# The head of the first convolution block: a transform spread over products, stores put in other queues, and the order of the last steps before the feed-forward part

## The chip, the cores and the metric

The kernel runs on one core of a Trainium2 chip. The metric is the device time of one execution in microseconds; lower is better. Of the kernel before there are three such times and one profiled execution with its trace. Five engines run side by side, each through its own list of instructions in order: TensorE (PE; its weight loads are shown as PEld), VectorE (DVE), ScalarE (ACT), GpSimd (POOL) and SyncE (SP), which does nothing but issue transfers. Transfers issued on SP run in one hardware queue (q1 in the profile), those issued on GpSimd in another (q0); both run on the same 16 DMA engines.

## The reference

```
x = A_u                                             # 2048 x 576
mod = (silu(c) @ w_mod) -> sa, ca, ga, sb, cb, gb   # six rows of 576
h = layernorm(x) * (1 + ca) + sa
dt = exp(log_dt); A = -exp(log_A_real) + 1j * A_imag; C = (C_real + 1j * C_imag) * dt
K[d, l] = 2 * Re( sum_n C[d, n] * exp(A[d, n] * dt[d] * l) )       # l = 0 .. 2047
y = causal convolution of K and h along the sequence (FFT of 4096) + h * D_skip
x = x + ga * y
h = layernorm(x) * (1 + cb) + sb
x = x + gb * ( relu(h @ w1) @ w2 )                  # 576 -> 4608 -> 576
```

All is float32. The inputs of K are scaled, so that K is not small.

## The kernel before, in words

The 2048 positions are cut into four blocks of 512 (block 0 to 3). A block's convolution is done with transforms of length 1024 over a block and its zero half; a later block adds the products of the earlier blocks' spectra. A block then goes through the second layernorm and the feed-forward part (FFN), in which each weight is split into a high part rounded to the matmul's format and a low part, the remainder.

**Head.** `KGen.first` makes K for block 0. The 576 channels are six groups of 96, g = 0 to 5, each in two halves u of 48. For each group it makes tables `W2` (powers of the step, 32 of them) and `W1` (16 values, made by `doubling`: four doublings by multiplication, the last of them of 8 to 16, m = 8, per half u), and `multiply(g)` runs 192 small matmuls on PE (2 halves x 96; each appears twice in the trace, since a float32 matmul is done in two passes), 32 x 16 each, into `kps`. ACT copies `kps` to `ke`; three groups make one half p of K's columns, which SP stores to `kd` and loads back in another order as `kt`. `W1`, `W2` and the factors `zs` are also stored to memory (`W1d`, `W2d`, `Zd`), where the later blocks' K is made from them (`rest`). `doubling`'s last additions (m = 8) run on GpSimd.

**Convolution of block 0**, `conv0`. The half p = 0 of the columns comes first, then p = 1. For each: `transform` multiplies h with a matrix of cosines and sines on PE (`ps_f`, eight matmuls, each copied by ACT to `ZU` or `Z1`), two butterflies on DVE make the spectrum `U` (`butterfly1` into a tile `W`, `butterfly2` out of it), the same is done for K (`ZK` or `WK`, then `K0` or `K1`), `product` on DVE multiplies the spectra (`Y`), two butterflies back make `V`, and `inverse` on PE (`ps_i`) with the matrix `gc` gives the time values, which DVE adds to x (`x2`) and takes statistics of (`bn_stats`). For p = 0 the second butterfly back is folded into the matmuls, 16 of them instead of 8, and for p = 1 the first butterfly of K is folded into PE (`transform1`, 16 matmuls with `fcK` and its negative `fcKn`). Before a transform of K the skip term `dsk` is added to one row of `kt`. The spectra are stored for later blocks by transfers issued on GpSimd (`Ud`, `Rd`).

**Modulation.** `mod_late` makes `sb`, `cb` and `gb`: for each a weight matrix `wm` of 1.3 MB is loaded on GpSimd's queue into one single buffer, 50 matmul passes (`mps`) use it, ACT copies the row, and PE turns it over (`mpt`). The next `wm` can only be loaded when the matmuls of the one before have read the buffer.

**End of the head.** `norm2` finishes the statistics, DVE and ACT make the normalised h, PE transposes it (`ps_t`), ACT and DVE scale it and split it into high and low parts (`xh`, `xl`, `xs`), and then the FFN's first matmuls (`hps`) run. The FFN's first weights come in as `r` on SP's queue; ACT makes their high part and DVE the low part (`w<-r` on both).

**FFN.** `ffn` walks through 36 slices of the hidden size for each of the four blocks: `first` (14 matmuls into `hps`), ACT and DVE split the result (`hh`, `hl`), `second` (14 matmuls into `acc`). Between them `step` puts in pieces of the next block's convolution, beginning with `rest`, whose tables come back on GpSimd's queue.

**What sets the order.** Instructions that are passed through `kept` or `v` while `pinned` is set stand on their engine in the order in which they are written (each gets a dependency on the one before it on that engine); all others are placed by the scheduler of the tile layer. A wait for another engine or a transfer is placed where data or a buffer needs it. `S(i, ...)` are four buffers for spectra, reused by name; the buffers of tag `kt` are two, which hold in turn `kt` of p = 0, the first and the second temporary `T` of `product`, and `kt` of p = 1.

Of the kernel before, what the change touches and what calls it, by code (L numbers as in the profile page):

```python
# [18 lines left out]
P = 128  # L19
L = 2048  # L20
D = 576
# [25 lines left out]
class KGen:  # L47
# [165 lines left out]
    def doubling(self, g):  # L213
# [4 lines left out]
        for i, m in enumerate((1, 2, 4, 8)):  # L218
# [5 lines left out]
            for u in (slice(0, 1), slice(1, 2)) if m > 2 else (slice(0, 2),):  # L224
# [11 lines left out]
                add = p if m == 8 else v  # L236
# [3 lines left out]
    def products(self, ps, W1, W2, u):  # L240

        for q in range(12):
            for dd in range(4):
                ch = dd * 12 + q
                for r in range(2):
                    self.nc.tensor.matmul(  # L246
                        ps[32 * dd : 32 * dd + 32, 12 * u + q, :],
                        W2[:, r, :, ch],
                        W1[:, u, :, r, ch],
                        start=(r == 0),  # L250
                        stop=(r == 1),
                    )

    def first(self, setup, mod, norm):
# [53 lines left out]
        def multiply(g):  # L308
            kps[g] = self.bank(f"kps_{g}")[:, :384].rearrange("p (q a) -> p q a", a=16)
            for u in range(2):  # L310
                self.products(kps[g], self.W1[g], W2s[g][u], u)
# [35 lines left out]
        multiply(4)  # L347
# [118 lines left out]
class Body:  # L466
# [108 lines left out]
    def mod_weights(self, w, col, eng):  # L575
        v = self.I["w_mod"]
        eng.dma_start(out=w[:, 0:4], in_=v[0:512, col].rearrange("(k p) c -> p k c", p=P))
        eng.dma_start(out=w[:64, 4], in_=v[512:576, col])

# [8 lines left out]
    def mod_late(self):  # L588

        nc, act = self.nc, self.nc.scalar.activation  # L590
# [3 lines left out]
        for i, nm in ((3, "sb"), (4, "cb"), (5, "gb")):  # L594
            w = cv.tile([P, 5, D], F32, tag="wm", bufs=1, name=f"wm_{nm}")
            self.mod_weights(w, slice(i * D, (i + 1) * D), nc.gpsimd)
# [3 lines left out]
            for group in (parts[:4], parts[4:]):  # L600
                for k in range(5):
                    kp = P if k < 4 else 64
                    for r, o, c, n in group:
# [3 lines left out]
                        )  # L607
            row = cv.tile([P, 2 * P], F32, tag="row", bufs=1, name=f"row_{nm}")
# [107 lines left out]
    def transform(self, src, fc, Z):  # L716

        nc = self.nc
        for n2 in (0, 2, 1, 3):
            for c in range(2):  # L720
                ps = self.cps.tile([P, 512], F32, tag="cps", bufs=self.nps, name="ps_f")
                o = ps[:, :PC].rearrange("p (a b) -> p a b", a=4)
                nc.tensor.matmul(o, fc[:, n2, c, :], src(n2), start=True, stop=True)  # L723
# [48 lines left out]
    def norms(self, st, kept):  # L772
# [3 lines left out]
        for i in range(4):  # L776
# [3 lines left out]
            if kept:  # L780
                self.tc.keep_in_program_order(sq)
            rs.append(mv)
# [156 lines left out]
    def norm2(self, s, x2, xp, st=None):  # L939
# [15 lines left out]
        for n2 in range(4):  # L955
            if s == 0 and n2 % 2 == 0:
                nc.vector.tensor_scalar(
                    h2[n2][:, :D], x2[:, n2], rs[n2][:, 0:1], rs[n2][:, 3:4],
                    op0=ALU.subtract, op1=ALU.mult,
                )  # L960
                nc.scalar.activation(h2[n2][:, D:], h2[n2][:, 512:D], AF.Copy)
                continue
            for a, b, c in ((0, D, 0), (512, D, D)):
                nc.scalar.activation(
                    h2[n2][:, c : c + b - a], x2[:, n2, a:b], AF.Identity,
                    scale=rs[n2][:, 3:4], bias=rs[n2][:, 4:5],
                )
# [22 lines left out]
    def conv0(self, ctx, c, kg, first, late):  # L990

        nc, I = self.nc, self.I
# [13 lines left out]

        def load(t, a):
            self.kept(nc.sync.dma_start(out=t, in_=a))

        def stores():  # L1010
            for dst, src in self.held:
                load(dst, src)
            self.held.clear()
# [3 lines left out]
        stores()  # L1017
# [409 lines left out]
```

## Time and profile before

| | |
|---|---|
| time, median of three runs | 1402.68 us (1402.18 to 1404.51) |
| the profiled execution's own time | 1402.97 us |
| span of its trace, first to last instruction | 1401.2 us |
| PE busy | 1233.9 us, 88% of the span |
| DVE busy | 878.3 us, 63% |
| ACT busy | 501.7 us, 36% |
| GpSimd busy | 196.0 us, 14% |
| the first FFN matmul (`hps`) begins | 236.98 us after the span's start |

The profile is read by stage, since the share of an engine over the whole span mixes the head, which has hardly any large matmuls, with the FFN. A row of the timeline gives the start in us, the duration of the merged instructions, the engine, the line, the operation with output and input, their number, and in brackets how long the engine sat idle before it and what ended that idle time. A row of the table by stretches gives the stretch, its length, busy time and number of instructions of PE, PEld, DVE, ACT and POOL, the clock that PE was granted (1.00 is full), the mean busy share of the 16 DMA engines, and GB/s.

### The profile page before, as it was taken

The numbers are of one execution on the slowest core, as the hardware profiler recorded it, in microseconds if no ns is written. First come the engines' busy times: TensorE is split into PE (matmuls) and PEld (weight loads), VectorE is DVE, ScalarE is ACT, GpSimd is POOL, SyncE is SP. The second block draws the span as 40 slices with busy tenths as digits, with TensorE's granted clock in tenths as the row PEclk, the third lists the DMA queues.
The fourth block names the chain that finished last, engine by engine and source line by source line (L and its number), as shares of the span: only waits on it lengthen the run. The fifth ranks groups of instructions, "written<-read, shape, count | busy, mean of one in ns | idle before, by whom it ended". The sixth has DMA issues, their size and how long they took to land. (4 is left out here: it accounts for less than half of the span.)

```text
span 1401.2 us, 25949 instructions
## 1 busy us (share of the span) xinstructions
PE 1233.9 (88%) x10600; PEld 978.8 (70%) x10600; DVE 878.3 (63%) x1352; ACT 501.7 (36%) x1006; POOL 196.0 (14%) x267
## 2 busy tenths in 40 slices
PE   5123677999999987899999989999999999999998
PEld 3123455777777776677777867777887878888886
DVE  5977968999875796658744987253989332101011
ACT  6975224222223412432233323533332353323231
POOL 1877311111111100021011010000000000000000
PEclk9555788999999999899999999999999999999999
DMA  6666778688886947499678995675989656666662
GB/s 190 236 239 217 264 260 314 230 296 310 287 304 219 334 156 282 160 324 376 222 245 314 331 361 174 189 233 174 384 303 325 198 160 204 204 195 198 199 197 78
DMA packets 135766, 346.36 MB, mean 247 GB/s; under 512 B 23456, under 2 KB 23744, under 8 KB 135648
## 3 DMA queue, kind: packets, MB, share of 16 engines
q1 hardware_dynamic: 108688, 222.75, 48.6%
q0 software_dynamic: 26672, 121.37, 23.7%
q8 instruction: 83, 1.36, 0.4%
q10 hardware_dynamic: 288, 0.59, 0.1%
q14 instruction: 35, 0.29, 0.1%
HBM read 263.26 MB, written 81.40 MB: 246 GB/s over the span
## 5 line engine op out<-in xcount | busy, mean ns | idle before, releaser
L1203 PE MATMUL acc<-hh,w 128*128 128x512 f32 x1296 | 429.1, 404 | 6.0 <-DVE w L488 6.0
L1178 PE MATMUL hps<-xh,w 128*128 128x512 f32 x1152 | 397.9, 405 | 0.0
L1184 DVE SCALAR_TENSOR_TENSOR hl<-hps,hh 128x512 fp32r<-128x512 f32 x144 | 98.9, 687 | 323.6 <-ACT hh L1183 323.4
L1203 PEld LDWEIGHTS acc<-hh,w 128*128 128x128 f32 x1296 | 244.5, 190 | 59.6 <-DVE w L488 7.5
L1203 PE MATMUL acc<-hl,w 128*128 128x512 f32 x720 | 280.3, 398 | 0.0
L1178 PEld LDWEIGHTS hps<-xh,w 128*128 128x128 f32 x1152 | 219.3, 191 | 48.2 <-ACT xh L981 0.7
L1178 PE MATMUL hps<-xl,w 128*128 128x512 f32 x576 | 230.0, 399 | 0.2 <-DVE xl L986 0.2
L1183 ACT ACTIVATE hh<-hps 128x512 fp32r<-128x512 f32 x144 | 86.0, 597 | 340.7 <-PE hps L1178 340.7
L1162 ACT ACTIVATE w<-r 128x576 fp32r<-128x576 f32 x144 | 98.7, 686 | 260.4 <-PE acc L1203 220.1
L1203 PEld LDWEIGHTS acc<-hl,w 128*128 128x128 f32 x720 | 136.1, 190 | 28.5
L1178 PEld LDWEIGHTS hps<-xl,w 128*128 128x128 f32 x576 | 110.1, 191 | 24.8 <-DVE xl L986 1.3
L246 PE MATMUL kps<-W,W 128*32 128x16 f32 x2304 | 40.0, 219 | 95.3 <-POOL W L59 59.9
L1153 ACT ACTIVATE w<-r 128x640 fp32r<-128x640 f32 x144 | 105.5, 733 | 39.6 <-DMA L1d<-w 30.4
L1178 PE MATMUL hps<-xs,w 128*128 128x512 f32 x288 | 103.7, 422 | 11.2 <-ACT w L1153 4.8
L246 PEld LDWEIGHTS kps<-W,W 128*32 128x32 f32 x2304 | 37.8, 150 | 98.5 <-POOL W L59 61.2
L421 PEld LDWEIGHTS kps<-W1r,W2r 128*32 128x32 f32 x3456 | 68.0, 146 | 31.1 <-issue 21.6
L488 DVE TENSOR_TENSOR Y<-Y,T 128x1152 f32<-128x1152 f32 x64 | 84.9, 1349 | 0.2
L421 PE MATMUL kps<-W1r,W2r 128*32 128x48 f32 (+2 forms) x3456 | 76.5, 238 | 8.0 <-issue 5.0
L1178 PEld LDWEIGHTS hps<-xs,w 128*128 128x128 f32 x288 | 54.1, 191 | 25.2 <-ACT w L1153 5.2
L488 DVE TENSOR_TENSOR w<-r,w 128x64 fp32r<-128x64 f32 (+2 forms) x108 | 58.2, 571 | 14.1 <-ACT w L1153 11.8
L724 ACT ACTIVATE Z<-ps_f 128x288 f32<-128x288 f32 x104 | 42.2, 409 | 68.1 <-PE ps_f L723 62.7
L931 PE MATMUL ps_i<-V,gc 128*128 128x288 f32 x136 | 43.2, 450 | 13.5 <-DVE x L488 10.1
(201 smaller groups left out, 1360.1 us busy)
## 6 DMA issues: line engine op xcount, KB each, us to landing
r<-in_w_dram SPq DMA_DIRECT2D x144, 320.0 KB, 3.7
r<-in_w_dram SPq DMA_DIRECT2D x144, 288.0 KB, 3.6
w<-L1d SPq DMA_DIRECT2D x108, 320.0 KB, 3.0
w<-L2d SPq DMA_DIRECT2D x108, 288.0 KB, 3.3
W2r<-W2d POOLq DMA_DIRECT2D x18, 1536.0 KB, 10.1
W2d<-W SPq DMA_DIRECT2D x12, 1536.0 KB, 7.7
Ua<-Ud POOLq DMA_DIRECT2D x15, 1152.0 KB, 10.8
W<-W1d POOLq DMA_DIRECT2D x18, 768.0 KB, 9.6
```

Source lines behind the costliest of these rows:

```text
L246: self.nc.tensor.matmul(ps[32 * dd : 32 * dd + 32, 12 * u + q, :], W2[:, r, :, ch], W1[:, u, :, r, ch], start=(r == 0), stop=(r == 1),)
L421: nc.tensor.matmul(ps[32 * dd : 32 * dd + 32, q, :], W2[:, r, :, ch], W1[:, :na, r, ch], start=(r == 0), stop=(r == 1),)
L488: return self.kept(self.nc.vector.tensor_tensor(*args, **kw))
L724: nc.scalar.activation(Z[:, n2, c], ps[:, :PC], AF.Copy)
L931: self.nc.tensor.matmul(ps[:, :PC], a, b, start=(i == 0), stop=(i == len(todo) - 1))
L1153: nc.scalar.activation(w[:, 0], r, AF.Copy)
L1162: nc.scalar.activation(w[:, 0:D], r, AF.Copy)
L1178: nc.tensor.matmul(ps, a, x, start=(i == 0), stop=(i == 13))
L1183: nc.scalar.activation(hh, ps, AF.Relu)
L1184: nc.vector.scalar_tensor_tensor(hl, ps, 0.0, hh, op0=ALU.max, op1=ALU.subtract)
L1203: nc.tensor.matmul(acc[i], a, x, start=(f == 0 and j in (0, 3, 6, 9, 12)), stop=(f == NF - 1 and j in (2, 5, 8, 11, 13)),)
```

## The change

All of it lies in the head and in the first weights of the FFN:

- `doubling` of the last group, g = 5: of the last additions (m = 8) those of the second half (u = 1) go from GpSimd to DVE.
- `multiply(4)` takes a generator `between`: the eight matmuls of K's transform for p = 0 (`ZK`) are put in pairs into the matmuls of group 4 at four places, instead of behind all of them.
- The stores: `W2d` of the last group go on SP behind the load of `kt` of p = 1 (before: ahead of it, behind `kt` of p = 0). `Zd` of the last group and the four `W1d` of groups 4 and 5 go from SP to GpSimd, behind the issue of the last `wm`.
- The loads: `fcKn` and `gcn` wait for the last matmul of `multiply(4)`; `gc` goes behind the load of x; `fcU` and `fcK` go behind the FFN's first weights, and the p = 1 transforms use the copies `early`, loaded before, instead of them.
- The first `wm` is loaded behind the load of `kt` of p = 1 (before: ahead of the butterflies of K0). The skip term of p = 1 is added by GpSimd instead of DVE.
- The spectra of p = 1 get other buffers: `V0` that of `U0`, `Z1` and `U1` the fourth, `K1` the third.
- The inverse of p = 0 and its additions to x stand ahead of the last two butterflies (`W`, `V1`), not behind them.
- The FFN's start is cut in two: the high parts of the first weights (`high1`, `high2`, on ACT) stand ahead of the last butterflies, the low parts (on DVE) behind the normalisation of h.
- The row of `gb` is copied by ACT behind the normalisation instead of ahead of it.

```diff
@@ doubling
-                add = p if m == 8 else v
+                add = p if m == 8 and (g < NG - 1 or u.start == 0) else v
@@ products
-    def products(self, ps, W1, W2, u):
+    def products(self, ps, W1, W2, u, between):
         for q in range(12):
+            if q % 6 == 3:
+                for _ in range(2):
+                    next(between, None)
             for dd in range(4):
...
-        multiply(4)
+        between = yield
+        multiply(4, between)
@@ mod_late
-            self.mod_weights(w, slice(i * D, (i + 1) * D), nc.gpsimd)
+            d = self.wm = self.mod_weights(w, slice(i * D, (i + 1) * D), nc.gpsimd)
+            if i == 3:
+                behind(d)
             yield
...
+            if nm == "gb":
+                yield
             row = cv.tile([P, 2 * P], F32, tag="row", bufs=1, name=f"row_{nm}")
@@ conv0
         kt = [self.load_kt(0, 0)]
-        stores()
-        for t, n in ((self.fcU, "fcu"), (self.fcK, "fck"), (self.gc, "gc")):
-            load(t, I[n])
-        for t, a in zip((fcKn, gcn), I["neg"]):
-            load(t, a)
...
-            self.v(ktv[0:1, 0, :, 0], ktv[0:1, 0, :, 0], dv, op=ALU.add)
+            add = nc.gpsimd.tensor_tensor if p else self.v
+            add(ktv[0:1, 0, :, 0], ktv[0:1, 0, :, 0], dv, op=ALU.add)
...
-        run(self.transform(src_K(0), early[:, 1], ZK))
+        ZKs = self.transform(src_K(0), early[:, 1], ZK, self.kept)
+        first.send(ZKs)
+        run(ZKs)
+        for t, a in zip((fcKn, gcn), I["neg"]):
+            d = load(t, a)
+            behind(d, kg.mm)
...
-        V = S(3, "V0")
+        V = S(0, "V0")
         run(self.butterfly1(Y, V))
         next(first, None)
         kt.append(self.load_kt(0, 1))
+        kt1 = self.ktd
+        sK1 = src_K(1)
         self.cps, self.nps = self.pool(c, "cpsb", space=PSUM), 4
-        Z1 = S(2, "Z1")
-        run(self.transform(lambda n2: hv[:, n2, :, 1], self.fcU, Z1))
+        Z1 = S(3, "Z1")
+        run(self.transform(lambda n2: hv[:, n2, :, 1], early[:, 0], Z1))
+        for dst, src in self.held[:2]:
+            load(dst, src)
         x2 = self.x2[0] = self.x2p[0].tile([P, 4, D], F32, tag="x2", bufs=1, name="x2_0")
         load(x2, I["x"][0].rearrange("n m d -> m n d"))
-        stores()
+        load(self.gc, I["gc"])
+        self.cv = self.pool(c, "cvm")
+        mod = self.mod_late(lambda d: behind(d, kt1))
         next(mod)
...
         run(self.product(Y, K1, U1, True))
-        W = S(2, "W")
-        run(self.butterfly1(Y, W))
-        V1 = S(1, "V1")
-        run(self.butterfly2(W, V1, 1))
...
         back(0, ops)
...
+        next(mod)
+        with tc.issue_after(self.wm.ins):
+            for dst, src in self.held[2:]:
+                nc.gpsimd.dma_start(out=dst, in_=src)
...
+        next(self.start)
+        W = S(3, "W")
+        run(self.butterfly1(Y, W))
+        V1 = S(1, "V1")
+        run(self.butterfly2(W, V1, 1))
...
         back(1, lambda n2: [(g(n2, c), V1[:, n2, c]) for c in range(2)])
```

**PE around the products of group 4** (`kps_2012` before and `kps_2004` now are group 4, `kps_2316` and `kps_2301` group 5; `ps_f<-kt,early` is K's transform for p = 0). Before:

```order
L723 MATMUL ps_f<-h_255,early 128x288 x8
L246 MATMUL kps_2012<-W_4_1810,W_8_1801 32x16 x96
L246 MATMUL kps_2012<-W_4_1810,W_9_1802 32x16 x96
L723 MATMUL ps_f<-kt,early 128x288 x8
L246 MATMUL kps_2316<-W_5_1872,W_10_1863 32x16 x96
L246 MATMUL kps_2316<-W_5_1872,W_11_1864 32x16 x96
L723 MATMUL ps_f<-h_255,fcU 128x288 x8
```

Now:

```order
L735 MATMUL ps_f<-h_255,early 128x288 x8
L250 MATMUL kps_2004<-W_4_1810,W_8_1801 32x16 x24
L735 MATMUL ps_f<-kt,early 128x288 x2
L250 MATMUL kps_2004<-W_4_1810,W_8_1801 32x16 x48
L735 MATMUL ps_f<-kt,early 128x288 x2
L250 MATMUL kps_2004<-W_4_1810,W_8_1801 32x16 x24
L250 MATMUL kps_2004<-W_4_1810,W_9_1802 32x16 x24
L735 MATMUL ps_f<-kt,early 128x288 x2
L250 MATMUL kps_2004<-W_4_1810,W_9_1802 32x16 x48
L735 MATMUL ps_f<-kt,early 128x288 x2
L250 MATMUL kps_2004<-W_4_1810,W_9_1802 32x16 x24
L250 MATMUL kps_2301<-W_5_1872,W_10_1863 32x16 x96
```

The eight transform matmuls have moved from between the groups into group 4, in four pairs, and group 5 follows group 4 directly.

**SP from the load of the first `kt` on.** Before:

```order
L1119 DMA kt<-kd_0_57 128x16x72
L1008 DMA W2d_75<-W_10_1863 128x4x768
L1008 DMA W2d_76<-W_11_1864 128x4x768
L1008 DMA Zd_99<-zs_1910 512x1x48
L1008 DMA Zd_100<-zs_1910 512x1x48
L1008 DMA fcU<-in_fcu_dram 128x1024
L1008 DMA fcK<-in_fck_dram 128x1024
L1008 DMA gc<-in_gc_dram 128x1024
L1008 DMA fcKn<-in_neg_dram 128x512
L1008 DMA gcn<-in_neg_dram 128x512
L358 DMA kd_1_58<-ke_1921 64x1152 x2
L1119 DMA kt<-kd_1_58 128x16x72
```

Now:

```order
L1153 DMA kt<-kd_0_57 128x16x72
L1029 DMA fcKn<-in_neg_dram 128x512
L1029 DMA gcn<-in_neg_dram 128x512
L365 DMA kd_1_58<-ke_1921 64x1152 x2
L1153 DMA kt<-kd_1_58 128x16x72
L1029 DMA W2d_75<-W_10_1863 128x4x768
L1029 DMA W2d_76<-W_11_1864 128x4x768
L1029 DMA x_0_2531<-in_x_dram 128x4x576
L1029 DMA gc<-in_gc_dram 128x1024
L1171 DMA r_2725<-in_w_dram 128x640
L1171 DMA r_2727<-in_w_dram 128x640
L1175 DMA r_2729<-in_w_dram 128x576
```

The two `W2d` stores and `gc` now stand behind the second `kt`, and the `Zd`, `fcU` and `fcK` are gone from here. The `W1d` stores, which stood behind the load of x on SP, now stand on GpSimd:

```order
L585 DMA wm_gb<-in_w_mod_dram 64x576
L1123 DMA Zd_99<-zs_1910 512x1x48
L1123 DMA Zd_100<-zs_1910 512x1x48
L1123 DMA W1d_85<-W_4_1810 128x2x768
L1123 DMA W1d_86<-W_4_1810 128x2x768
L1123 DMA W1d_87<-W_5_1872 128x2x768
L1123 DMA W1d_88<-W_5_1872 128x2x768
L386 DMA W_0_2925<-W1d_77 128x2x768
L387 DMA Zr_2926<-Zd_89 128x192
L388 DMA W2r_2924<-W2d_65 128x4x768
```

On GpSimd they stand between the last `wm` and the first loads of `rest`, which before followed each other.

More of the change, by code (lines that the diff above doesn't have):

```diff
@@ L1072, in conv0 @@
         WK = S(1, "WK")
-        run(self.transform1(src_K(1), self.fcK, fcKn, WK))
+        run(self.transform1(sK1, early[:, 1], fcKn, WK))
         next(mod)
@@ L1240, in ffn @@
         low1(1)
+        high1(0)
+        high2(0)
+        high1(1)
+        yield
         split1(0)
```

106 lines of the change are left out of this document (63 added, 43 removed).

## The prediction

> **What bounds the kernel now.** I read the table by stretches first, to find where PE is not the limit, and then the timelines of that place.
>
> ```profile
> 64.00:89.00 25.00, 12.79 (x766) 12.15 (x760) 19.05 (x46) 16.80 (x34) 22.53 (x30) 0.50 0.51 192
> 148.00:162.00 14.00, 4.83 (x267) 4.53 (x268) 13.79 (x27) 0.00 (x0) 6.65 (x7) 0.59 0.96 365
> 195.00:219.00 24.00, 18.96 (x116) 13.64 (x116) 16.22 (x22) 5.68 (x15) 2.93 (x5) 1.00 1.03 398
> 300.00:400.00 100.00, 98.46 (x1549) 79.10 (x1548) 94.30 (x101) 24.26 (x45) 12.85 (x19) 1.00 0.85 297
> ```
>
> In the FFN PE is the limit (98.46 of 100 us), and its work does not change. So the time follows the instant at which the FFN starts, as long as nothing behind it is late. In the head it is DVE that is nearly always busy (13.79 of 14 us), and at 195 to 219 the DMA engines are full at 398 GB/s. DVE's timeline of the head:
>
> ```profile
> 160.91 4.78 DVE L488 TENSOR_TENSOR W<-ZU 128x576 f32<-128x576 f32 x4
> 169.39 1.43 DVE L488 TENSOR_TENSOR W<-ZK 128x576 f32<-128x576 f32 x2 [0.54 <-ACT ZK L724]
> 171.89 1.43 DVE L488 TENSOR_TENSOR W<-ZK 128x576 f32<-128x576 f32 x2 [1.08 <-ACT ZK L724]
> ...
> 176.18 2.62 DVE L488 TENSOR_TENSOR Y<-K,U 128x1152 f32<-128x1152 f32 x2
> ...
> 180.09 1.36 DVE L488 TENSOR_TENSOR Y<-Y,T 128x1152 f32<-128x1152 f32 x1
> ...
> 184.15 2.76 DVE L488 TENSOR_TENSOR V<-Y 128x576 f32<-128x576 f32 x4
> 188.38 1.43 DVE L488 TENSOR_TENSOR W<-Z 128x576 f32<-128x576 f32 x2 [1.47 <-ACT Z L724]
> 191.74 1.43 DVE L488 TENSOR_TENSOR W<-Z 128x576 f32<-128x576 f32 x2 [1.93 <-ACT Z L724]
> ...
> 196.02 0.44 DVE L488 TENSOR_TENSOR kt<-kt,dsk 1x288 f32<-1x288 f32 x1
> 204.07 2.90 DVE L488 TENSOR_TENSOR K<-WK 128x576 f32<-128x576 f32 x6 [7.61 <-ACT WK L763]
> ...
> 214.99 2.76 DVE L488 TENSOR_TENSOR W<-Y 128x576 f32<-128x576 f32 x4
> ...
> 220.60 0.45 DVE L488 TENSOR_TENSOR x<-ps_i,x 128x288 f32<-128x288 f32 x1
> ...
> 224.01 2.28 DVE L488 TENSOR_TENSOR w<-r,w 128x640 fp32r<-128x640 f32 x4
> ...
> 229.32 0.41 DVE L1103 BATCH_NORM_STATS2 st<-x 128x6 f32<-128x288 f32 x1
> 234.13 0.81 DVE L977 TENSOR_SCALAR xf<-ps_t,m_cb,m_sb 128x512 f32<-128x512 f32 x1 [2.25 <-PE ps_t L972]
> ```
>
> The chain is DVE's own work and five waits: 0.54 + 1.08 for `ZK`, 1.47 + 1.93 for `Z1`, 7.61 for `WK`, 12.6 us in sum. The last one is a loop: the skip term is added only at 196.02, behind U1 on DVE, and only then can PE transform K.
>
> **Step 1, the products on PE.** The rows from PE, and those that follow from it on SP:
>
> ```profile
> 67.83 2.18 PE L246 MATMUL kps<-W,W 128*32 128x16 f32 x128 [1.39 <-issue]
> ...
> 150.31 0.30 PE L246 MATMUL kps<-W,W 128*32 128x16 f32 x2 [4.18 <-POOL W L59]
> ...
> 157.76 2.18 PE L246 MATMUL kps<-W,W 128*32 128x16 f32 x127 [4.15 <-issue]
> ...
> 165.39 6.02 PE L723 MATMUL ps_f<-kt,early 128*128 128x288 f32 x16
> 171.34 4.03 PE L246 MATMUL kps<-W,W 128*32 128x16 f32 x249
> ...
> 181.21 0.43 PE L246 MATMUL kps<-W,W 128*32 128x16 f32 x7 [2.12 <-issue]
> ```
> ```profile
> 182.19 1.12 SPq L358 DMA_DIRECT2D kd<-ke  x2
> 185.33 0.38 SPq L1119 DMA_DIRECT2D kt<-kd  x1
> ```
>
> Group 4 takes 15.1 us (150.31 to 165.39), of which 6.5 are work (384 passes at 2.18/128); after each 128 passes PE stands without a releaser. That gap is 4.15 us here, with the DMA engines at 0.96, and 1.39 at 67.83, where they are at 0.51. I read it as PE's instructions arriving by DMA. Now `W2d`, `Zd`, `fcU`, `fcK` and `gc`, some 5 MB by their shapes, leave this stretch, so a lot of 128 should cost about 3.6 us (2.18 + 1.39), and the eight transform matmuls (6.0 us) fill the gaps: the first 140 passes by 153.6, then 4.2 + 6.0 of work, group 4 and `ZK` done at about 164 instead of 171.4. Group 5 then takes its 10.3 us (171.34 to 181.64) and ends at 174.3, 7.3 us earlier. Bounds: 5 us of gain if only the transform's 6.0 hide, 9 if gaps vanish; none if the gaps stay and the pairs add to them. The Trainium skill ("Runtime: NRT & Kernel Launch", Instruction fetch mechanics) has fetching in blocks of 256 instructions, mostly hidden. The lots of 128 matmuls with 128 weight loads agree with the block; the 4.15 us do not agree with "hidden".
>
> **Step 2, DVE to U1.** The moved additions cost DVE two of 0.5 us, about 1.1 in all. They give back the slow `W<-ZU`: 4.78 us where the same shape takes 2.76 (184.15), because GpSimd ran at the same time:
>
> ```profile
> 159.48 4.92 POOL L59 TENSOR_TENSOR W<-T,T 128x384 f32<-128x384 f32 x4 [6.09 <-issue]
> ```
>
> Half of GpSimd's four are gone, so 2.0 less. The `ZK` waits (1.6) go. Y starts at 176.18 - 2.5 = 173.7 (a gain between 1 and 3). The copy `cb` moves within the same path. `Z1` no longer waits for the buffer that V0's butterfly reads, and its matmuls follow group 5 (from 174.3), so the 1.47 + 1.93 go too: U1 ends at 196.02 - 5.9 = 190.1.
>
> **Step 3, K1.** The new waits first: SP now waits for group 4's last matmul ahead of `fcKn`; behind it stand `gcn` and the stores of `ke`, which need group 5 anyway, so it costs nothing unless group 4 ends after group 5's copy, which cannot be. GpSimd waits for `kt` of p = 1; behind it stand the first `wm` and U1's store, which pay in step 4.
>
> `kt` of p = 1 is issued 3.7 us after group 5 (181.64 to 185.33): 178.0. It also needs its buffer, the first `T`, read by the row at 180.09: 181.4 - 2.5 = 178.9 now. So this, not PE, decides, which makes step 1 forgiving by a microsecond.
>
> ```profile
> kt<-kd SPq DMA_DIRECT2D x2, 576.0 KB, 4.1
> wm_sb<-in_w_mod_dram POOLq DMA_DIRECT2D x1, 1152.0 KB, 6.1
> wm_cb<-in_w_mod_dram POOLq DMA_DIRECT2D x1, 1152.0 KB, 10.8
> ```
> ```profile
> 196.56 0.72 PE L760 MATMUL ps_f<-kt,fcK 128*128 128x288 f32 x2 [2.14 <-DVE kt L488]
> ...
> 207.55 0.66 PE L931 MATMUL ps_i<-V,gc 128*128 128x288 f32 x2
> ...
> 216.20 0.65 PE L931 MATMUL ps_i<-V,gcn 128*128 128x288 f32 x2
> ...
> 221.10 5.84 PE L931 MATMUL ps_i<-V,gc 128*128 128x288 f32 x16 [4.25 <-DVE x L488]
> ...
> 231.77 3.17 PE L972 MATMUL ps_t<-ident,h 128*128 128x128 f32 x16 [1.75 <-ACT h L961]
> ...
> 236.98 1.22 PE L1178 MATMUL hps<-xs,w 128*128 128x512 f32 x2 [0.27 <-DVE xs L984]
> ```
>
> Landing 183.0, half a microsecond more beside the store of K0; the addition on GpSimd 0.4 (DVE's row) to 1.2 (4.92/4, four times the work with 128 partitions): I take 0.8, so 184.3. K1 follows the transform's start by 7.5 (196.56 to 204.07): 191.8, behind U1's 190.1. The 7.61 becomes 1.7. K1 comes 12.3 us earlier than before, and Y ends at 191.8 + 10.9 = 202.7.
>
> **Step 4, what the moved transfers take back.** From 183 on SP's queue holds `W2d` (two of 128 x 4 x 768 floats, 3.15 MB), x (1.18), `gc` (0.52), and the inverse of p = 0 cannot start before `gc`. On GpSimd's queue run `wm_sb` (1.3 MB, issued behind the addition, so from about 186.5) and U1's store. Shares of the two queues in a full stretch (195 to 210):
>
> ```profile
> q1 hardware_dynamic: 1237, 3.44, 61.2%
> q0 software_dynamic: 588, 2.49, 40.5%
> ```
>
> SP alone moves 1.4 MB until 186.5, and the other 3.46 MB at 58% of 398 GB/s take 15: `gc` is there at 201.5 (195 at the full rate). The Trainium skill ("DMA: Bandwidth & Descriptors", Queues, rings and completion order) has each engine take turns between queues by packet; with equal halves it would be 204. The inverse takes 8.6 (207.55 to 216.85 less a wait of 0.7): 210.1, so the last addition and its statistics end at 211, where DVE alone would be done at 202.7 + 3.4. That is about 5 us taken back. Then the butterflies, 5.6 (214.99 to 220.60): 216.6; the inverse of p = 1 starts 1.5 before their end and takes 5.8: 220.9, last statistics at 221.9 instead of 229.7. Here the low parts (2.28 at 224.01) no longer stand ahead of the additions; behind h they fill DVE's wait of 2.25 ahead of `xf` (if it shrinks, up to 2.3 come back).
>
> The tail is as before, so `hps` starts at 236.98 - 7.8, say 229.5. At nothing I cost: the high parts on ACT (three rows of 0.7, in a stretch where ACT is busy 5.7 of 24 us; without that cover 2 us), the row of `gb` behind h (ACT waits for the transposes there; without it 0.6 us), and `fcU` and `fcK`, which no one needs before block 1. **Sum:** 12.3 up to K1, less 5 for `gc`, and about 0.5 from the order of additions and low parts, with nothing behind: 7.5 us. The profiled execution, 1402.97, becomes 1395.5; the median of the three runs is 0.3 below that execution, less than I can resolve.
>
> **The rivals.** (a) *The transfers do not hold*: x and `gc` are there by 202. Then additions end at 206, butterflies at 211.7, statistics at 217: 12.5 us, 1390.5. For it: 195 at the full rate; against: the 1.03 at 195 to 219 with fewer bytes.
>
> (b) *The modulation's single buffer becomes the bound.* `wm_sb` 185 + 10.8 = 195.8, its 2.6 us of work, `wm_cb` behind U1's store on the same queue to about 212, 2.6 again, `wm_gb` 6.1: 221, and its matmuls end at 224 on PE, just ahead of the transposes (231.77 - 7.5 = 224.3). Four microseconds more in any landing go to the end: 1399.5. The skill's "DMA: Bandwidth & Descriptors" (Issuing engines are not separate DMA queues) says that a change of queue saves issue time only. The row of 10.8 against 6.1 agrees.
>
> (c) *The products do not get faster*: the gaps stay, group 5 ends at 180, `kt` is added at 190, K1 starts at 197.5, and `W2d` and `gc` move back with it, to 207: statistics at 227.5, about 1.5 us of gain, 1401.5. The skill's "hidden" fetch would speak for this, since transfers would then not be the cause; the gaps' growth with the DMA share speaks against.
>
> (d) *Slower*: `rest` loses its start. Its first loads now stand behind 3.3 MB of `W1d` and `Zd` on GpSimd's queue, and its first DVE work stands in DVE's order ahead of `hl` of the next slice, so PE's second products would wait. At 42% of 398 GB/s (167) these stores take 20 us from 220, the first tables (0.9 MB) 5 more: 245, against about 236 when DVE comes to them. From 243.5 on, where DVE began `rest` before, it is a loss: with the second table of 1.5 MB late as well some 3 us, 1406. Against it: the FFN's own traffic is below half at 300 to 400 (297 GB/s in all), so 231 to 234 is likelier.
>
> **How the numbers follow.** Chances: forecast 0.56 (its own range 1392.5 to 1398.5), (a) 0.14, (b) 0.14, (c) 0.08, (d) 0.08. A measurement of this kernel tells about 0.2%, 2.8 us, from no change, so faster means below 1399.9: nearly all of the forecast, (a), and half of (b): 0.77. Same: the other half of (b), (c): 0.15. Slower: 0.08. The range is 1390 (with (a)) to 1401.5 (with (c)).
>
> **What would show it.** Right: `kps` gaps near 1.4 us after 150 and group 5 ending at 173 to 176; `W<-ZU` near 2.8 us; K1 at 191 to 193 with a wait under 3; `ps_i` of p = 0 starting with `gc`, near 201; last statistics near 222; `hps` near 229.5. Wrong: gaps still of 4 us (c), `mps_gb` ending behind h (b), DVE idle ahead of `T<-W,Zr` in the first slices (d), or a later idle stretch of PE that takes the gain back.

## The result, and the profile after

The change makes the kernel slower: 1411.12 us (median of 8 runs, 1404.84 to 1419.22) against 1402.43 us for the kernel before (8 runs, 1399.19 to 1404.51). The ratio is 1.0054, with a 95% interval of 1.0034 to 1.0075. The prediction was 1395.5 us. The profiled execution took 1411.59 us, with a span of 1409.8 us.

Four rows of DVE's timeline in the head of the changed kernel answer to those of the prediction:

```profile
160.81 2.75 DVE L495 TENSOR_TENSOR W<-ZU 128x576 f32<-128x576 f32 x4
...
196.84 2.90 DVE L495 TENSOR_TENSOR K<-WK 128x576 f32<-128x576 f32 x6 [7.78 <-ACT WK L775]
...
214.91 0.46 DVE L1115 BATCH_NORM_STATS2 st<-x 128x6 f32<-128x288 f32 x1
...
225.38 0.40 DVE L1115 BATCH_NORM_STATS2 st<-x 128x6 f32<-128x288 f32 x1
```

The first row starts 0.1 us from where it started before, so the instants of the two executions can be compared from here on. (This execution had begun group 4's products 1.5 us earlier, at 148.84 instead of 150.31, and the two additions that DVE took over, 1.34 us, used that up.) The last statistics are reached 3.9 us earlier than before (229.32), where 7.8 had been forecast. PE's timeline has the rest of the story:

```profile
173.88 0.41 PE L250 MATMUL kps<-W,W 128*32 128x16 f32 x6 [2.67 <-issue]
...
186.35 1.33 PE L772 MATMUL ps_f<-kt,early 128*128 128x288 f32 x2 [6.29 <-POOL kt L1039]
...
203.41 6.10 PE L945 MATMUL ps_i<-V,gc 128*128 128x288 f32 x12 [1.76 <-DMA gc<-in_gc_dram]
...
233.24 0.73 PE L1220 MATMUL hps<-xs,w 128*128 128x512 f32 x2
...
252.58 1.43 PE L1220 MATMUL hps<-xs,w 128*128 128x512 f32 x2 [11.50 <-ACT hh L1225]
```

The FFN starts at 233.24, 3.7 us earlier than before (236.98). Then PE stands for 11.5 us ahead of the third slice's matmuls. The releaser is the first Relu `hh`, and ACT's timeline shows why that Relu is late:

```profile
236.29 0.67 ACT L1198 ACTIVATE w<-r 128x576 fp32r<-128x576 f32 x1
250.29 0.68 ACT L1198 ACTIVATE w<-r 128x576 fp32r<-128x576 f32 x1 [13.33 <-DMA r<-in_w_dram]
250.88 0.58 ACT L1225 ACTIVATE hh<-hps 128x512 fp32r<-128x512 f32 x1
```

In ACT's order the high part of `w2` of slice 2 stands ahead of the first Relu, and its raw weight `r` is still in flight. The kernel before has the same order, but there the weight had landed:

```profile
240.61 1.24 ACT L1162 ACTIVATE w<-r 128x576 fp32r<-128x576 f32 x2
242.25 0.60 ACT L1183 ACTIVATE hh<-hps 128x512 fp32r<-128x512 f32 x1 [0.40 <-PE hps L1178]
```

So the first Relu goes from 242.25 to 250.88: 8.6 us later. From there both kernels take the same time: 1401.2 - 242.3 = 1158.9 us before, 1409.8 - 250.9 = 1158.9 after. So in these two executions the loss lies between 233 and 251.

SP's timeline says when the weight was issued. `r1(2)`, `r1(3)` and `r2(2)` are the raw weights of slices 2 and 3; `L1d` and `L2d` are the stores of the low parts:

```profile
228.59 0.33 SPq L1171 DMA_DIRECT2D r<-in_w_dram  x1
228.96 2.00 SPq L1299 DMA_DIRECT2D L1d<-w  x1
231.00 0.96 SPq L1299 DMA_DIRECT2D L2d<-w  x1
232.06 0.51 SPq L1299 DMA_DIRECT2D L1d<-w  x1
232.68 0.38 SPq L1171 DMA_DIRECT2D r<-in_w_dram  x1
233.15 5.09 SPq L1175 DMA_DIRECT2D r<-in_w_dram  x2
```

The raw weights have two buffers each, and a buffer comes free when DVE has made the low part from it. These low parts moved from 224.01 to behind h:

```profile
227.72 2.28 DVE L495 TENSOR_TENSOR w<-r,w 128x640 fp32r<-128x640 f32 x4
```

So `r2(2)` is issued at 233.15. Before it was at 227.73. Of these 5.4 us, 3.7 are the move of the low parts; the rest comes mostly from the three stores in between, which now take 3.5 us to issue instead of 1.2. Before, `r2(2)` also needed half the time to land. The first row below is from the table of issues of the kernel before, the second from that of the changed one (queue and operation, count, KB, us from issue to landing):

```profile
r<-in_w_dram SPq DMA_DIRECT2D x1, 288.0 KB, 8.3
```

```profile
r<-in_w_dram SPq DMA_DIRECT2D x1, 288.0 KB, 17.1
```

What it met on the way shows in the changed kernel's GpSimd timeline, the loads of `rest` for the next block, all of them issued before 233:

```profile
219.43 3.04 POOL L1123 DMA_DIRECT2D W1d<-W  x4
225.32 0.73 POOL L386 DMA_DIRECT2D W<-W1d  x1 [2.85 <-PE ps_i L945]
...
226.62 0.92 POOL L388 DMA_DIRECT2D W2r<-W2d  x1
...
228.79 0.75 POOL L388 DMA_DIRECT2D W2r<-W2d  x1
```

In the kernel before, the first of these loads was issued at 227.49 and the two `W2r` at 228.77 and 230.77, so `r2(2)` at 227.73 stood ahead of most of them. Now it stands behind all of them, and behind the four stores.

### The profile page after: what moved, and what is told of

It reads as the page before. It is cut to its first block, busy times and chain, and to the rows that moved or that the text cites. A ratio compares the mean times of both kernels' runs of the same rounds, so it can differ in the third digit from the quotient of the medians.

```text
span 1409.8 us, 25952 instructions
## 1 busy us (share of the span) xinstructions
PE 1238.4 (88%) x10600; PEld 982.3 (70%) x10600; DVE 882.8 (63%) x1353; ACT 502.3 (36%) x1006; POOL 199.3 (14%) x272
## 4 chain that ended last, share of the span: by engine, by line
PE 62%; DVE 20%; DMA 11%; issue 3%; ACT 2%; POOL 1%; SPq 0%; ACTq 0%; DVEq 0%; POOLq 0%
PE hps L1220 24%; PE acc L1245 24%; PE kps L428 5%; DVE Y L495 4%; DVE T L495 4%; DVE W L495 3%; PE ps_f L735 2%; PE ps_i L945 2%; DMA Ud<-U 2%; DMA r<-in_w_dram 2%; DMA L1d<-w 2%; DMA Ua<-Ud 1%; DMA gc<-in_gc_dram 1%; DVE k L125 1%; PE kps L250 1%
## 5 line engine op out<-in xcount | busy, mean ns | idle before, releaser
L1220 PE MATMUL hps<-xs,w 128*128 128x512 f32 x288 | 103.0, 420 | 21.1 <-ACT hh L1225 11.5
L945 PE MATMUL ps_i<-V,gc 128*128 128x288 f32 x136 | 44.2, 461 | 12.3 <-DVE x L495 6.4
## 6 DMA issues: line engine op xcount, KB each, us to landing
Ua<-Ud POOLq DMA_DIRECT2D x15, 1152.0 KB, 10.5
W<-W1d POOLq DMA_DIRECT2D x18, 768.0 KB, 10.2
```

The lines of the kernel that those rows point to most:

```text
L945: self.nc.tensor.matmul(ps[:, :PC], a, b, start=(i == 0), stop=(i == len(todo) - 1))
L1220: nc.tensor.matmul(ps, a, x, start=(i == 0), stop=(i == 13))
```

## The experiments

"Theory A" below is the chain just read from the rows: the low parts, moved behind h, free the raw weights' buffers late; `r2(2)` is then issued behind the transfers on GpSimd's queue; and ACT's order lets the first Relu wait for it. The rivals put the loss on the moved stores alone, or on bandwidth in general. Executions differ by some us in the head already, so the column to compare first is the distance from the first `hps` to the first `hh` in each run's trace.

| kernel | ratio to before, 95% interval | `r2(2)` issued | landed after | first `hps` | first `hh` | distance |
|---|---|---|---|---|---|---|
| before | 1 | 227.73 | 8.3 | 237.0 | 242.3 | 5.3 |
| changed | 1.0054 (1.0034 to 1.0075) | 233.15 | 17.1 | 233.2 | 250.9 | 17.7 |
| low parts early again | 1.0005 (0.9975 to 1.0036) | 224.87 | 16.4 | 231.7 | 241.9 | 10.2 |
| no stores | 1.0004 (0.9987 to 1.0022) | 228.60 | 15.4 | 228.6 | 244.6 | 16.0 |
| stores on SP | 1.0018 (0.9997 to 1.0038) | 229.04 | 15.7 | 233.3 | 245.4 | 12.1 |
| before, low parts late | 1.0032 (1.0012 to 1.0052) | 230.09 | 17.3 | 231.8 | 248.0 | 16.2 |
| changed, third buffers | 0.9971 (0.9951 to 0.9992) | early | | 237.4 | 243.3 | 5.9 |
| changed, Relu first | 0.9980 (0.9958 to 1.0002) | 230.15 | 17.0 | 227.8 | 233.1 | 5.3 |
| low parts early, third buffers | 0.9979 (0.9956 to 1.0001) | early | | 231.3 | 239.4 | 8.1 |
| before, third buffers | 1.0000 (0.9979 to 1.0021) | early | | 236.3 | 241.6 | 5.3 |

### The low parts back ahead of the last inverse

```diff
         next(self.start)
         ...
         self.cv = self.pool(c, "cvb")
+        next(self.start)
         back(1, ...)
         ...
             if w == -1:
-                next(self.start)
```

> The changed kernel with one part undone: the low parts of the FFN's first weights (DVE, 2.28 us) stand again ahead of the additions of the second inverse, not behind the normalised h. Theory A (the new weights r are issued too late, since SP waits for those low parts, and then stand behind GpSimd's transfers; ACT has r ahead of hh, so PE stops): the r of slice 2 is issued at about 226 instead of 233, lands by 237 instead of 250, PE's stop of 11.5 us in the second slice falls to under 3, the first hps is up to 1 us later, and the time is 1398 to 1402, at or below the kernel before. Theory B (the W1d and Zd stores on GpSimd's queue alone hold everything behind them, whenever the weights are issued): stop of 8 us or more, 1408 to 1411.

Measured: 1404.51 us, ratio 1.0005. ACT's wait shrinks from 13.33 to 5.71:

```profile
241.27 0.68 ACT L1198 ACTIVATE w<-r 128x576 fp32r<-128x576 f32 x1 [5.71 <-DMA r<-in_w_dram]
```

On SP the issue of `r2(2)`, the first of the two merged here:

```profile
224.87 11.98 SPq L1175 DMA_DIRECT2D r<-in_w_dram  x2
```

`r2(2)` is issued 8.3 us earlier than in the changed kernel but still takes 16.4 us to land. Here the stores (issued from 215.59 on) and the first two loads of `rest` (224.08 and 224.79) lie ahead of it, but both `W2r` (225.37 and 227.54) are issued behind it. So its place ahead of most of `rest` did not save it. PE still stops for 3.87 us, where theory A expected under 3, and the time is above the expected 1398 to 1402. The place of the low parts is a large part of the loss, but the crowded queue alone still leaves a wait.

### The stores left out

This kernel leaves out the stores of `Zd` and `W1d` of the last groups; `rest` reads the tables of other groups instead, so that the loads stay as many.

```diff
-        with tc.issue_after(self.wm.ins):
-            for dst, src in self.held[2:]:
-                nc.gpsimd.dma_start(out=dst, in_=src)
...
-    W0 <- strips(k.W1d[h], 2);  Z <- k.Zd[h]
+    W0 <- strips(k.W1d[h if h < 8 else h - 4], 2);  Z <- k.Zd[h if h < 10 else h - 4]
```

> The changed kernel without the six stores Zd and W1d on GpSimd (left out; the later blocks read the tables of other groups instead, so part of the later blocks' convolution kernel is computed from wrong tables; all loads keep their number and size). Theory A: 3.3 MB less ahead of the late weights, at 400 GB/s 8 us, so PE's stop falls from 11.5 to 3 to 5 us, time 1401 to 1404. Theory B: the stop vanishes, under 1 us, time 1397 to 1400. A theory in which neither counts (order of instructions on PE or ACT alone): 1409 to 1413.

Measured: 1404.27 us, ratio 1.0004. The distance is 16.0 us, and ACT's wait is 2.2 us shorter than in the changed kernel:

```profile
244.04 0.68 ACT L1195 ACTIVATE w<-r 128x576 fp32r<-128x576 f32 x1 [11.13 <-DMA r<-in_w_dram]
```

So the stores by themselves are not what holds the weight; the rival that puts it all on them falls. Theory A had its price of the stores wrong too: it expected PE's stop at 3 to 5 us, and it is 9.25. Without the stores the loads of `rest` start at 222.01 and fill the queue as well. What this execution gains is mostly its earlier `hps` (228.6 instead of 233.2); the run with the Relu first, further down, has the changed kernel's head and reaches `hps` as early, so that need not come from the stores.

### The stores on SP

```diff
         load(self.gc, I["gc"])
+        for dst, src in self.held[2:]:
+            load(dst, src)
...
-        with tc.issue_after(self.wm.ins):
-            for dst, src in self.held[2:]:
-                nc.gpsimd.dma_start(out=dst, in_=src)
```

> The changed kernel with Zd and W1d again on SP, behind gc and ahead of the first weights r. Theory A: the late weights meet 3.3 MB less on GpSimd's queue: stop of 3 to 5 us; but wm_sb and wm_cb share their time with the stores, so the first hps comes 0 to 4 us later: 1402 to 1406. Theory B: stop under 1 us, 1398 to 1402 by the same shift.

Measured: 1407.69 us, ratio 1.0018. ACT waits 7.81 us for `r` (the row at 244.78 of its timeline), less than with the stores on GpSimd, but the weight takes 15.7 us to land. PE stops for 5.95 us, where theory A expected 3 to 5. The time is above the ranges of both theories. It lies between the changed kernel and the kernel before, and the interval holds no change, so this run alone decides nothing.

### The kernel before with the low parts late and nothing else of the change

```diff
-        run(self.norm2(0, x2, self.xp[0], st))
+        for w in self.norm2(0, x2, self.xp[0], st):
+            if w == -1:
+                next(self.start)        # the low parts; high1, high2 stay ahead
```

The edit also fixes the places of the instructions that make the normalised h on DVE and ACT, as the changed kernel does.

> The kernel before with one part of the change alone: the FFN's first high parts ahead of the second inverse, the low parts behind the normalised h. The stores stay on SP. Theory A: SP issues the r of slice 2 at about 233 instead of 228, behind the 4.9 MB that rest loads on GpSimd's queue at 227 to 231, so it lands at 243 to 246 instead of 236, and PE stops for 3 to 6 us in the second slice: 1404 to 1408, slower than before. Theory B: no stop, the same as before or up to 2 us faster, since the additions of the second inverse no longer wait for the low parts: 1400 to 1403.

Measured: 1409.41 us, ratio 1.0032 with an interval that excludes 1. This part of the change, without the others, is enough to make the kernel slower. ACT's wait:

```profile
247.37 0.68 ACT L1166 ACTIVATE w<-r 128x576 fp32r<-128x576 f32 x1 [11.24 <-DMA r<-in_w_dram]
```

And PE's, behind it:

```profile
249.66 0.77 PE L1188 MATMUL hps<-xs,w 128*128 128x512 f32 x1 [9.40 <-ACT hh L1193]
```

Here the first load of `rest` is issued at 224.61 and `r2(2)` at 230.09, so the weight stands behind those loads, and lands late, without any moved store.

### Third buffers for the raw weights

```diff
-    r1[g] = ff.tile(..., tag="r1", bufs=2);  r2[g] = ff.tile(..., tag="r2", bufs=2)
+    r1[g] = ff.tile(..., tag="r1", bufs=3);  r2[g] = ff.tile(..., tag="r2", bufs=3)
...
-        load_r1(0); load_r1(1); load_r2(0)
+        for g in range(3): load_r1(g)
+        for g in range(3): load_r2(g)
...
-                if g + 2 < n: load_r1(g + 2)
-                if g + 1 < n: load_r2(g + 1)
+                if g + 3 < n: load_r1(g + 3)
+                if g and g + 2 < n: load_r2(g + 2)
```

> The changed kernel with a third buffer for each of the raw weight tiles r1 and r2 and three of each loaded at the start, so that the weights of slice 2 no longer wait for the low parts. Theory A (the low parts behind h release the raw weights' buffers 5 us late, and ACT's order then holds the first Relu behind a weight that is still in flight): PE's wait of 11.5 us ahead of the second hps goes to under 3, the first hh starts near 238 to 240 instead of 250.9, and the end moves with it: about 1398 to 1400, 0.2 to 0.4% faster than the kernel before. Rival (bandwidth: the bytes of the GpSimd queue hold whatever is issued in that stretch): the earlier loads are held as well, the first hh stays above 245, 1405 or more.

Measured: 1398.72 us, ratio 0.9971 (0.9951 to 0.9992). This version is faster than both kernels. The wait ahead of the first Relu is gone:

```profile
241.62 1.24 ACT L1198 ACTIVATE w<-r 128x576 fp32r<-128x576 f32 x2
243.28 0.60 ACT L1225 ACTIVATE hh<-hps 128x512 fp32r<-128x512 f32 x1 [0.41 <-PE hps L1220]
```

The first `hh` itself is later than the expected 238 to 240, because this execution ran some 4 us late from before the change's first step (its butterfly of `ZU` starts at 164.7 us); the distance, 5.9 us, is that of the kernel before.

### The first Relu ahead of the late weight

Loads and buffers are those of the changed kernel; only ACT's order (and DVE's, for the low part) is another.

```diff
             act = nc.scalar.activation(w[:, 0:D], r2[g], AF.Copy)
+            if g == 2:
+                behind(act, hs[0])        # hs: the first hh and hl
...
             low = v(w[:, D:640], ...)
+            if g == 2:
+                behind(low, hs[1])
```

> The changed kernel with one thing of the order altered: on ACT the high part of w2 of slice 2 stands behind the first Relu, and on DVE its low part behind the first hl. The loads stay as late as they are. If the order on ACT and DVE alone makes the stop (the weights are needed only 15 us later): first hh near 238 to 240, no wait over 3 us on PE behind it, 1398 to 1400. If PE needs the late weights themselves: the first hh is early, but PE stands for some 8 us ahead of an hps or a second product of slice 1 or 2, and the time stays at 1408 to 1411.

Measured: 1398.84 us, ratio 0.9980 (0.9958 to 1.0002). The weight is as late as ever, but the first Relu no longer stands behind it:

```profile
233.11 0.60 ACT L1239 ACTIVATE hh<-hps 128x512 fp32r<-128x512 f32 x1 [0.98 <-PE hps L1233]
...
247.17 0.68 ACT L1207 ACTIVATE w<-r 128x576 fp32r<-128x576 f32 x1 [9.58 <-DMA r<-in_w_dram]
```

While the weight is on its way, PE has the first matmuls of another slice and the second ones of slice 0 to do; its longest wait from the first `hps` up to 262 us is 2.95 us instead of 11.50. The distance of 5.3 us in the table flatters this run, though, since the weight now holds the third Relu instead of the first:

```profile
248.39 0.58 ACT L1239 ACTIVATE hh<-hps 128x512 fp32r<-128x512 f32 x1
```

A fairer count runs from the start of the butterfly of `ZU` to the fourth Relu: 98.3 us before, 107.0 in the changed kernel, 97.2 here and 95.7 with the third buffers. So the loss needs both: a weight that lands late, and an order in which an engine that others wait for stands in front of it. By this count the third buffers take away some 11 us and the order some 10; the ratios of the runs say much the same (0.83% and 0.74% of 1402 us, 11.6 and 10.4).

### Third buffers with the low parts early, and in the kernel before

The edit is that of the third buffers, made in the kernel with the low parts early and in the kernel before.

> The third buffers of the raw weights together with the low parts back ahead of the last inverse. Theory A: as the run with the buffers alone, first hh near 237 to 240, 1397 to 1400; whatever this differs from that run is the price of the low parts' place by itself (up to 2.3 us of DVE). Rival (bandwidth): 1404 to 1405 as with the low parts early and two buffers.

> The kernel before with the third buffers and early loads alone. Theory A: its first Relu stands 5.3 us behind the first hps, of which up to 3.5 may be the same wait for a weight; so 1399 to 1403, and the gain of the other runs against this one is what the head alone gives. If the buffers by themselves give 4 us or more, the gain of the other runs isn't the change's.

Measured: 1399.81 us, ratio 0.9979 (0.9956 to 1.0001), and 1401.71 us, ratio 1.0000 (0.9979 to 1.0021). The buffers give the kernel before nothing that can be measured, so what the run with third buffers gains, 0.3%, comes from the change's work in the head. With third buffers no difference between the two places of the low parts can be measured either (0.9971 and 0.9979, with intervals that overlap): as DVE work their price is small, as it was put. The distance of 8.1 us in the first of the two traces ends with a wait for PE's `hps` (1.09 us), not for a weight.

### Keeping PE at work ahead of two waits

These runs ask where the rest of the forecast gain went. In the changed kernel's table by stretches, PE's granted clock (the third number from the end) falls to a half in the first pairs of K1's transform, and to 0.57 in the inverse of p = 0:

```profile
186.00:190.00 4.00, 3.65 (x8) 2.64 (x9) 3.06 (x6) 0.41 (x1) 1.65 (x3) 0.50 1.03 411
202.00:206.00 4.00, 2.59 (x6) 1.90 (x7) 3.96 (x4) 1.47 (x2) 1.08 (x2) 0.57 1.04 416
206.00:210.00 4.00, 4.00 (x11) 2.89 (x10) 2.52 (x4) 1.97 (x2) 0.00 (x0) 0.57 1.03 395
210.00:214.00 4.00, 4.00 (x19) 3.08 (x17) 1.84 (x4) 0.00 (x0) 0.00 (x0) 1.00 0.94 352
```

Matmuls whose results nobody reads were added to the kernel with third buffers: 16 behind the transform of `Z1`, and some ahead of the inverse of p = 0.

```diff
+        def warm(n):
+            ps = ...                     # a PSUM bank
+            for _ in range(n):
+                self.kept(nc.tensor.matmul(ps, early[...], hv[...]))   # later runs: gcn, gcn
...
         run(self.transform(..., Z1))
+        warm(16)
...
+        warm(6)                          # later runs: 9
         back(0, ops)
```

> The kernel with the third buffers of the raw weights, and 22 added matmuls whose results nobody reads, which only keep PE at work where it waits: 16 behind the transform of Z1 (ahead of kt of p = 1) and 6 ahead of the inverse of p = 0. Theory C (PE stands still ahead of both, so its granted clock falls to a half and the next matmuls take twice as long): the first pairs of K1's transform take 0.65 us instead of 1.17, the inverse of p = 0 takes 8.0 us instead of 11, and from the start of the butterfly of ZU to the first hps it is about 69 us instead of 72.7; the time about 1395.5 to 1397, that is 2 to 3 below the run with the buffers alone. Rival: the transfers (wm_gb, gc) hold the stretch anyway, or the added matmuls delay the real ones: 72 to 73 us to the first hps, 1398.7 or more.

> As the run before it, and with the order in which ACT takes the high part of w2 of slice 2 behind the first Relu (on DVE its low part behind the first hl). Theory A: with the third buffers that weight lies ready, so the order no longer matters: the same time as without it, within 1.5 us. If it is 2 us or more faster, the order cost something beside the late weight.

Measured: 1407.14 us, ratio 1.0045 (1.0018 to 1.0073), and with the Relu first 1409.14 us, ratio 1.0053 (1.0032 to 1.0075). Slower, for a reason that neither theory had. The load of x on SP in the first of the two:

```profile
199.63 0.37 SPq L1029 DMA_DIRECT2D x<-in_x_dram  x1
```

And PE's rows:

```profile
184.44 0.65 PE L774 MATMUL ps_f<-kt,early 128*128 128x288 f32 x2
...
210.44 5.12 PE L945 MATMUL ps_i<-V,gc 128*128 128x288 f32 x12 [10.84 <-DMA gc<-in_gc_dram]
```

The added matmuls read h, and the load of x goes into h's space, so x, and `gc` behind it, were issued only when the second lot of them was done (in the changed kernel x is issued at 182.21). K1's transform does run at full clock (0.65 us a pair). Whether the Relu's order matters with third buffers can't be read from the second run, which stands too near the first (2 us between medians, with intervals that overlap) and shares its fault. The same with matmuls that read `gcn`:

> The run with the third buffers and added matmuls once more, but the added matmuls (16 ahead of kt of p = 1, 9 ahead of the inverse of p = 0; nobody reads their results) read gcn and not h, whose space the load of x waits for: in the run before, x and gc were issued 13 us late for that reason. Theory C (the half clock costs the inverse of p = 0 some 3 us): gc is issued as with the buffers alone, the inverse of p = 0 takes 8.0 us instead of 11, the first hps stands 69 to 70 us behind the start of the butterfly of ZU instead of 72.7, 1395.5 to 1397. Rival (the transfers hold the stretch): mps_sb is done earlier, wm_cb is issued earlier on GpSimd's queue and takes the packets that x and gc would have had, gc lands later by as much, and the time is 1398 to 1401.

> The same added matmuls in the kernel with the low parts early and the third buffers. Theory C: 2 to 3 us below that kernel's 1399.8, about 1397; here the low parts (2.3 us of DVE) lie ahead of the last additions, in a wait for PE if the inverse of p = 1 runs at half clock and on the path if it doesn't, so the gain may be smaller than in the other run. Rival as there: 1399 to 1402.

Measured: 1401.32 us, ratio 0.9999 (0.9981 to 1.0018), and 1403.43 us, ratio 1.0004 (0.9983 to 1.0025). From the first of the two, PE's rows and then DVE's:

```profile
205.37 4.15 PE L1037 MATMUL ps_w<-gcn 128*128 128x288 f32 x16
209.36 3.07 PE L945 MATMUL ps_i<-V,gc 128*128 128x288 f32 x12
```

```profile
211.50 0.46 DVE L495 TENSOR_TENSOR x<-ps_i,x 128x288 f32<-128x288 f32 x1 [3.47 <-PE ps_i L945]
```

The inverse's first twelve passes take 3.07 us instead of 6.10, and there is no wait for `gc` any more, which had landed at 204.8. But the added matmuls end only at 209.4, and now the inverse waits for them and DVE for the inverse. So the half clock is shown to be what doubles these rows; in the run with the Relu first, where the clock was 1.00, the same twelve passes take 3.15 us without any added matmul. Both times lie just above the ranges of both theories. That keeping PE at work pays is not shown, and a lot of a better length was not tried.

## Why the prediction was wrong

**The step that failed** is the last of step 4: "behind h they fill DVE's wait of 2.25 ahead of `xf`" and "The tail is as before ... with nothing behind". The low parts were priced as 2.3 us of DVE, and as that they cost nothing that the runs can tell. But they also release the raw weights' two buffers, and on SP `r1(2)`, three stores and `r2(2)` stand behind that release. The prediction never named what the moved instructions release, nor what ACT's order puts behind the weight that comes last. This term was missing from the sum; it measured 12.4 us (the distance from `hps` to `hh`, 17.7 instead of 5.3), against a gain of 3.7 ahead of it.

Point by point:

- **Step 1** hit its instant in part by luck: group 5 was forecast to end at 174.3 and ends at 173.88 + 0.41 = 174.29. But this execution began group 4 1.5 us earlier, and from there to the end of group 5 it takes 25.5 us, where 24.0 was forecast and 31.3 measured before. The pairs fill group 4's gaps, as forecast. Group 5 does not keep its 10.3 us: it follows group 4 directly and has three gaps (0.89, 1.85 and 2.67 us) where it had two (1.56 and 2.12) behind the eight transform matmuls. The forecast gap of 1.4 was the smallest of its stretch, which also has gaps up to 3.23.
- **Step 2** held: `W<-ZU` 2.75 us (2.8 expected), no wait for `ZK` or `Z1` left, U1 done at 189.1 (190.1), with the 1.5 us of the early start in it.
- **Step 3** was mis-sized by 5.0 us: K1 at 196.84 instead of 191.8, with the wait at 7.78 instead of 1.7. The addition on GpSimd takes 2.26 us where 0.8 was chosen from a range of 0.4 to 1.2 (the row below), and it starts 0.5 us later than forecast, since `kt` waited for the stores to `kd`, which landed at 179.51, and not for the buffer of the first `T`. K1 follows the transform's start by 10.5 instead of 7.5 us, since its first six pairs ran at half clock.

```profile
184.04 2.26 POOL L1039 TENSOR_TENSOR kt<-kt,dsk 1x288 f32<-1x288 f32 x1 [10.88 <-DMA kt<-kd]
```

- **Step 4**, the head's end: `gc` at 203.41 (201.5 forecast), the inverse of p = 0 takes 11.0 us (8.6, its first half at a clock of 0.57), so the last statistics stand at 225.8 instead of 221.9. These two terms, 1.9 + 2.4, are the missing gain in this execution's head; K1's 5.0 lie beside them, since DVE is done with Y at 207.7, while the inverse lasts to 214.4. SP's share of the bytes, which the sum put at 58%, was 4.16 of 6.52 MB from 186.5 to 203.4, so it is not what made `gc` late; what did stays open. The inverse's 11.0 us differ by the execution: it takes 8.0 in the run with the Relu first, which has the same head. The terms of the sum (12.3, 5 and 0.5) give 7.8, which the prediction rounds to 7.5. The third-buffer run, 4 us below the kernel before, is the best measure of what the head is worth when nothing behind it takes it back.
- **The rivals.** (a) and (c) did not happen. (b) did not either: `mps_gb` follows the last inverse without a wait. (d), the slower one, with a chance of 0.08, came out with the right sign, but by another mechanism. It had the crowd, the 3.3 MB of stores and the tables on GpSimd's queue (though the runs without moved stores show that the tables alone are enough), and the wrong victim: it let `rest` wait for its tables, while in fact the FFN's own weights, on the other queue, waited. Of the prediction's signs of being wrong, the last one came: a later idle stretch of PE, 11.50 us, that took the gain back.

## What to carry to other kernels

An instruction that moves takes with it what it releases: before a moved step is priced by its engine time, look for the buffers that it frees and for the transfers that stand behind these. Here the same weight landed in 8.3 us when little stood in the other queue, and in 15 to 17 us when that queue had several MB to move; so look where in an in-order engine's list the instruction stands that needs the late one, and what stands behind it. A third buffer or another order on that one engine was worth 10 to 12 us here, and the change's own gain, some 0.2 to 0.3%, became visible only then.

## What the runs showed of the hardware

**Two busy queues shared by packets, not by bytes.** In the changed kernel between 236 and 244 us, when both queues had work, they moved nearly the same number of packets (queue, packets, MB, share of the engines):

```profile
q0 software_dynamic: 437, 2.30, 70.6%
q1 hardware_dynamic: 440, 0.97, 31.3%
```

The tables' packets on GpSimd's queue are 5.3 KB each, the weights' on SP's 2.2 KB, so SP gets 30% of the bytes. The prediction took a fixed share of 58% for SP from one stretch. The Trainium skill ("DMA: Bandwidth & Descriptors", Queues, rings and completion order) has each engine take turns between queues by packet: the trace agrees, 437 to 440 here, and 323 to 322 between 194 and 200 us.

**A transfer that was issued beside a full queue moved nothing at first.** Between 229 and 233 us the changed kernel's SP had issued `r1(2)`, at 228.59, and stores behind it, and still nothing of its queue moved (the only other row is one packet of instructions):

```profile
q0 software_dynamic: 265, 1.45, 99.1%
```

It was the same the other way round: `wm_sb`, issued on GpSimd at 186.25 beside SP's full queue, had moved 4 packets by 192, against 722 of SP's from 186.5 on. In the kernel before, `r1(2)` was issued at 224.85 with the other queue idle, and had landed 3.4 us later. Why the turns begin so late, no run here shows.

**PE's clock after a wait.** Behind an idle time of 6.29 us a pair of K1's transform takes 1.17 us, and 0.65 where PE had been kept at work. The Trainium skill ("TensorE: Matmul & The Clock Gate", Part 1) has PE at half its clock after an idle window of some 3.4 us, with a window that runs free of the kernel. The trace agrees with the half (0.50). The inverse of p = 0 had a clock of 0.57 in the changed kernel's profile and 1.00 in the same stretch of the run with the Relu first, which has the same head, so it differs from one execution to the next: a gain of a few us that rests on it can't be counted on.

**A small addition on GpSimd** of one partition with 288 values took 2.26 us in the changed kernel and 1.18 to 2.75 us over the runs, always beside DVE's butterflies, against 0.44 on DVE.
